# The opening of a convolution by Fourier tables: where k is turned, and on which engines the tables are made

## The chip, the cores and the metric

The kernel runs on one core of a Trainium2 chip. A core has five engines, each with a queue of its own: TensorE (PE, matrix products; PEld is its weight load), VectorE (DVE), ScalarE (ACT), GpSimd (POOL) and SyncE (SP, which here only issues transfers). They work on the on-chip memory SBUF (128 partitions) and on PSUM, where matrix products land. The metric is device time in microseconds for one execution, the median of several.

## The reference, cut to what matters

A forward pass of four layers and its gradients are computed, for 2048 positions and 512 channels. Two layers are a convolution A over the positions and two a dense layer B with GELU:

```python
def _A_ref(q, k, v, shift_k, ssm_k, ssm_D):
    k_pad = jnp.pad(k, ((0, 0), (ks - 1, 0), (0, 0)))
    k_shift = jnp.zeros_like(k)
    for t in range(ks):                       # ks = 4
        k_shift = k_shift + k_pad[:, t:t + S, :] * shift_k[:, ks - 1 - t][None, None, :]
    kv = k_shift * v
    # kv and ssm_k are padded to 4096, multiplied as spectra, and transformed back: y
    y = y + kv * ssm_D[None, None, :]
    return q * y

x = A_q
x = x + _A_ref(_layernorm(x), A_k, A_v, ...)
x = x + _B_ref(_layernorm(x), B_w1, ...)
x = x + _A_ref(_layernorm(x), A_k, A_v, ...)
x = x + _B_ref(_layernorm(x), B_w1, ...)
```

The gradients of all inputs but B_x are returned too. k, v and ssm_k are the same in both A layers, so y is computed once.

## The kernel before, in words

`phase_conv_forward` computes y, `phase_mlp` runs the layers forward and back, and `conv_backward` with `weight_grads` does the rest. The change lies in the first 85 us, in `phase_conv_forward`.

The Fourier transforms are products with tables of sines and cosines. The 2048 frequencies are split into five `GROUPS` by residue, and each group has its own folding of the input (`Fold.streams`), so that a group needs two or four streams of 512 columns times 128x128 pieces of table.

The opening has these steps, in the order of the code:

- **h chunks** (`h_chunk`, called from the loop at L518, four times). ssm_k, called h, is turned (transposed by a product with the identity) 128 channels at a time. One half goes to `ha_ps` in PSUM and is copied to `hA` by VectorE; the other to `hb_ps` and is copied to `hR` by ScalarE (L513). The four middle taps go through `hs_ps` to `hsp`. Ahead of each chunk `sin_of` (L175) makes one quarter of the table `tabN`. It works on 1024 columns at a time: a phase (frequency times position plus a shift, in integers), an AND with 8191, and a sine on ScalarE (L186). The phase of the first 1024 columns is made on GpSimd (L182) and that of the second on VectorE; both ANDs are on VectorE. The three buffers of `tab_u` hold the phases until their sine is done.
- **wdiag** (L526): sixteen diagonal matrices with the shift taps, on VectorE.
- **hB** (L531 to L533): `hR` is reversed by eight products with the anti-diagonal `anti` into `hr_ps`, and copied to `hB` by ScalarE.
- **tap rows** (L534 to L541): the table rows `sp5` for the middle taps and ssm_D, by ten calls of `sin_of` on 5 partitions and 128 columns each (five groups, cosine and sine).
- **fold of h** (L545 to L547): one row of `hB` is set to zero, then `Fold` and the streams of groups 0 and 1, `sth`, on VectorE.
- **k slices** (`k_slice`, L468, called four times at L583). 512 positions of k, loaded to `kns`, are turned by four sets of four products into `kt_ps` (two buffers of one PSUM bank, tag `kt`), each copied to `kT` by ScalarE (L475). Small copies on GpSimd (L477, L479) join the edges of neighbouring slices.
- **shift products** (`ks_slice`): k_shift by 64 products of `kT` with `wdiag` per slice, into `ks_ps`, copied by ScalarE to `ksb` (L492), stored, and multiplied by v on VectorE into `kv`, which is kept in `y_res`. Between them come `h_group`(0) and (1), the spectrum of h for the first two groups, the streams of the later groups, and `tabF_part`, which makes the table `tabF` for kv with the same `sin_of`. After them the other h groups run, with the turning of both tables in between (`table_turns`), and the spectrum of kv follows.

The h groups (`fwd_group`) use `sp_ps`, two buffers of two PSUM banks each (tag `sp`). Each of their results sums a real and an imaginary part; the first block of group 0 needs `sp5` and `altq` in its imaginary part (`extra`, L549). [...]

What sets the order: `nc = Ordered(...)` (L415) keeps the instructions of TensorE and VectorE in the order in which the code writes them, in this phase. L55 is the line of that wrapper, so all their rows have L55 in the profile and are told apart by their tiles. The order on ScalarE, GpSimd and SyncE, and of every engine in `phase_mlp`, is written by a planner, which takes the instruction that it reckons ready, the earlier one in the code first. Every engine then works its queue in that fixed order.

Of the kernel before, what the change touches and what calls it, by code (L numbers as in the profile page):

```python
# [11 lines left out]
ACT = mybir.ActivationFunctionType  # L12
ALU = mybir.AluOpType
BF16 = mybir.dt.bfloat16
F32 = mybir.dt.float32
I32 = mybir.dt.int32
P = 128
# [54 lines left out]
def ssm_kernel(ctx, tc: tile.TileContext, aps: dict):  # L72
# [28 lines left out]
    dram.gp = {li: drampool.tile([P, NFC, S], BF16, name=f"gp{li}_d") for li in (1, 3)}  # L101
    res.wstack = ExitStack()
    phase_conv_forward(nc, tc, dims, consts, dram, res, aps)
    flip_rows(nc, dram.goB, aps["grad_out"].flatten_outer_dims(), 511)
    with ExitStack() as res.gystack:
# [17 lines left out]
GROUPS = [(0, 0, 2), (4, 2, 2), (2, 4, 4), (1, 8, 4), (3, 12, 4)]  # L123


def iota_f32(nc, pool, shape, pattern, base, mult, name):
    ti = pool.tile(shape, I32, name=name + "_i")
    nc.gpsimd.iota(ti, pattern=pattern, base=base, channel_multiplier=mult)
    tf = pool.tile(shape, F32, name=name)
    nc.vector.tensor_copy(out=tf, in_=ti)  # L130
    return tf
# [40 lines left out]
SIN_SCALE = -(2.0 * math.pi / 8192.0) * (1.0 - SIN_EPS)  # L172


def sin_of(nc, consts, pool, out, krow, pv, shift, np_=P):  # L175
    n = krow.shape[-1]
    us = []
    for c0 in range(0, n, 1024):
        w = min(1024, n - c0)
        u = pool.tile([P, 1024], I32, name="tab_u", tag="tab_u", bufs=3)[0:np_, 0:w]  # L180
        eng = nc.gpsimd if c0 == 0 else nc.vector
        eng.tensor_scalar(out=u, in0=krow[:, c0:c0 + w], scalar1=pv, scalar2=float(shift), op0=ALU.mult, op1=ALU.add)  # L182
        us.append((c0, w, u))
    for c0, w, u in reversed(us):
        nc.vector.tensor_single_scalar(out=u, in_=u, scalar=8191, op=ALU.bitwise_and)
        nc.scalar.activation(out=out[:, c0:c0 + w], in_=u, func=ACT.Sin, scale=SIN_SCALE, bias=consts.pibias[0:np_, :])  # L186
# [105 lines left out]
def fwd_group(nc, psum, tab, st, g, out, extra=None, m0=0, m1=None, c0=0):  # L292
    k1, base, n = GROUPS[g]
    for mt in range(m0, n if m1 is None else m1):
        cols = slice((base + mt) * P - c0, (base + mt + 1) * P - c0)
        ps = psum.tile([P, 2, 512], F32, name="sp_ps", tag="sp", bufs=2)
        R, Z = [], []
        for qt in range(2):
            C, S = tab[:, 0, qt, cols], tab[:, 1, qt, cols]
            q = slice(qt * 512, (qt + 1) * 512)  # L300
            if k1 in (0, 4):
                R.append((C, st["e"][:, q]))
                Z.append((S, st["o"][:, q]))
            else:
                R += [(C, st["er"][:, q]), (S, st["oi"][:, q])]
                Z += [(C, st["nei"][:, q]), (S, st["orr"][:, q])]
        if extra is not None:
            er, ez = extra(g, mt, st)
            R += er
            Z += ez  # L310
        for b, lst in ((0, R), (1, Z)):
            for i, (a, r) in enumerate(lst):
# [97 lines left out]
def phase_conv_forward(ctx, nc, tc, dims, consts, dram, res, aps):  # L410
    S, D, NT, ND = dims.S, dims.D, dims.NT, dims.ND
# [3 lines left out]
    nc = Ordered(nc, tc, ("tensor", "vector"))  # L415
    tt = nc.vector.tensor_tensor
    psum = ctx.enter_context(tc.tile_pool(name="cf_ps", bufs=1, space=bass.MemoryType.PSUM))
# [8 lines left out]
    tabF = tabs.tile([P, 2, 2, 2048], BF16, name="tabF")  # L426
# [4 lines left out]
    gp = gen.enter_context(tc.tile_pool(name="cf_gen", bufs=1))  # L431

    KA, KB, KW = 16, 272, 544
    kns = []
# [9 lines left out]
    krow = gp.tile([P, 2048], F32, name="krow")  # L444
# [4 lines left out]
    kT = gp.tile([P, ND, 4, KW], BF16, name="kT")  # L449
# [8 lines left out]
    hsp = gp.tile([5, D], BF16, name="hsp")  # L458
# [4 lines left out]
    pvh = iota_f32(nc, gp, [P, 2], [[2 * P, 2]], -511, 2, "pvh")  # L463
    pvn = iota_f32(nc, gp, [P, 2], [[2 * P, 2]], 0, 2, "pvn")
    tabN = gp.tile([P, 2, 2, 2048], BF16, name="tabN")
    sp5 = gp.tile([5, 5, 2, P], BF16, name="sp5")
    altq = gp.tile([P, P], BF16, name="altq")
    def k_slice(i):  # L468
        for h in range(4):
            ps = psum.tile([P, ND, P], F32, name="kt_ps", tag="kt", bufs=2)  # L470
            for cc in range(ND):
                nc.tensor.matmul(ps[:, cc, :], lhsT=kns[i][:, h, cc * P:(cc + 1) * P],
                                 rhs=consts.ident if h < 2 else consts.anti, start=True, stop=True)
            c0 = KA + P * h if h < 2 else KB + P * (3 - h)
            nc.scalar.activation(out=kT[:, :, i, c0:c0 + P], in_=ps, func=ACT.Identity)  # L475
        for j in range(1, 4):
            nc.gpsimd.tensor_copy(out=kT[:, :, i, KB + 255 + j:KB + 256 + j], in_=kT[:, :, i, KA + 256 - j:KA + 257 - j])  # L477
            if i < 3:
                nc.gpsimd.tensor_copy(out=kT[:, :, i + 1, KA - j:KA + 1 - j], in_=kT[:, :, i, KB + j - 1:KB + j])  # L479
# [20 lines left out]
    def h_chunk(cc):  # L500
        b = cc * S
        for m in range(2):
            c = slice(m * 512 + cc * P, m * 512 + (cc + 1) * P)
            ps = psum.tile([P, 4, P], F32, name="ha_ps", tag="kt", bufs=2)
            for i in range(4):
                nc.tensor.matmul(ps[:, i, :], lhsT=hN[:, b + 512 * i + m * P:b + 512 * i + m * P + P], rhs=consts.ident,
                                 start=True, stop=True)
            nc.vector.tensor_copy(out=hA[:, :, c], in_=ps)
            ps = psum.tile([P, 4, P], F32, name="hb_ps", tag="ks", bufs=2)
            for i in range(4):  # L510
                t0 = b + 512 * (i or 4) - m * P - P + 1
                nc.tensor.matmul(ps[:, i, :], lhsT=hN[:, t0:t0 + P], rhs=consts.ident, start=True, stop=True)
            nc.scalar.activation(out=hR[:, :, c], in_=ps, func=ACT.Identity)  # L513
        ps = psum.tile([4, P], F32, name="hs_ps", tag="kt", bufs=2)
        nc.tensor.matmul(ps, lhsT=hN[:, b + 256:b + S:512], rhs=consts.ident, start=True, stop=True)
        nc.vector.tensor_copy(out=hsp[0:4, cc * P:(cc + 1) * P], in_=ps)

    for cc in range(ND):  # L518
        qt, f = cc // 2, cc % 2
        sin_of(nc, consts, gp, tabN[:, f, qt, :], krow, pvn[:, qt:qt + 1], 2048 * (1 - f))  # L520
        h_chunk(cc)
    wshf = gp.tile([P, ND, 4], F32, name="wshf")
    nc.vector.tensor_copy(out=wshf, in_=wsh)
    for cc in range(ND):
        for j in range(4):
            nc.vector.tensor_scalar(out=wdiag[:, cc, j, :], in0=consts.ident, scalar1=wshf[:, cc, j:j + 1],  # L526
                                    scalar2=None, op0=ALU.mult)

    for m in range(2):
        for i in range(4):  # L530
            ps = psum.tile([P, 512], F32, name="hr_ps", tag="ks", bufs=2)  # L531
            nc.tensor.matmul(ps, lhsT=consts.anti, rhs=hR[:, i, m * 512:(m + 1) * 512], start=True, stop=True)
            nc.scalar.activation(out=hB[:, i, m * 512:(m + 1) * 512], in_=ps, func=ACT.Identity)  # L533
    pi5 = gp.tile([5, 1], I32, name="pi5")  # L534
    nc.vector.memset(pi5, 0)
    nc.gpsimd.iota(pi5[0:4, :], pattern=[[0, 1]], base=512, channel_multiplier=1024)
    pv5 = gp.tile([5, 1], F32, name="pv5")
    nc.vector.tensor_copy(out=pv5, in_=pi5)
    for gi, (k1, base, n) in enumerate(GROUPS):
        for f in range(2):  # L540
            sin_of(nc, consts, gp, sp5[:, gi, f, :], krow[0:5, base * P:(base + 1) * P], pv5, 2048 * (1 - f), np_=5)  # L541
    nc.vector.memset(sp5[:, 0, 1, 0:1], 1.0)
    nc.vector.memset(altq, 0.0)
    nc.vector.tensor_copy(out=altq[:, 0:1], in_=consts.alt)
    nc.vector.memset(hB[0:1, :, 0:512], 0.0)  # L545
    fh = Fold(nc, foldp, hA, hB, True, xpool=res.xpool)
    sth = [fh.streams(GROUPS[0][0]), fh.streams(GROUPS[1][0])]  # L547

    def extra(g, mt, st):  # L549
        R = [(sp5[:, g, 0, :], hsp)]  # L550
        Z = [(sp5[:, g, 1, :], hsp)]
        if g == 0:
            Z = []
            if mt == 0:
                Z = [(sp5[:, g, 1, :], hsp), (altq, st["e"][:, 0:512]), (altq, st["e"][:, 512:1024])]
        return R, Z

    tabIt = {}
# [16 lines left out]

    def tabF_part(x):
        qt, f = x // 2, x % 2
        sin_of(nc, consts, gp, tabF[:, f, qt, :], krow, pvh[:, qt:qt + 1], 2048 * (1 - f))
        if f:
            nc.vector.tensor_copy(out=tabF[:, 1, qt, 0:1], in_=consts.alt)  # L580

    for i in range(4):
        k_slice(i)  # L583
    for i in range(4):
        ks_slice(i)
        if i < 2:
            h_group(i)
        if i in (1, 3):
            sth.append(fh.streams(GROUPS[(i + 3) // 2][0]))
        tabF_part(i)  # L590
# [881 lines left out]
```

## Time and profile before

| | |
|---|---|
| median of 10 runs | 927.1 us (924.51 to 935.75) |
| the profiled execution | 928.26 us |
| its span, first to last instruction | 926.5 us |
| mean granted TensorE clock | 0.94 |
| PE busy | 774.8 us (84%) |
| VectorE busy | 733.5 us (79%) |
| ScalarE busy | 568.3 us (61%) |
| GpSimd busy | 150.9 us (16%) |

How to read the lines shown: a timeline row has the start in us, the time from the first to the last instruction of the row, the engine, the line of the code, the operation, the tile written and the tiles read, shapes, and xN for N instructions merged. In brackets stands how long the engine had been idle and what released it. A row of the table by stretches has, for each engine, the busy time in that stretch and the number of instructions, then the granted TensorE clock, the share of the transfer engines and the transfer rate. The windows of such a table cut off at a time, so neighbouring rows add up.

### The profile page before, as it was taken

The page shows a single profiled execution, that of the slowest core. Times are in us where ns is not written, and L with a number is a line of the kernel's source. Part 1 is how long each engine was busy: PE and PEld are TensorE (multiplying, and loading weights), DVE is VectorE, ACT ScalarE, POOL GpSimd, SP SyncE. Part 2 cuts the span into 40 slices and gives each one's busy share as a digit, 9 for nine tenths or more (in the row PEclk, how much of TensorE's full clock was granted, in tenths as well). Part 3 has the DMA queues.
Part 4 walks back from the last instruction along what each step waited for, and adds up shares of the span by engine and source line. Part 5 has one row for each costly group of instructions (what it writes and reads, how often), then busy time and mean ns, then how long its engine had stood idle before and what let it go on. Part 6 is the DMA issues. An engine that isn't in the chain of part 4 may idle for free. (4 is left out here: it accounts for less than half of the span.)

```text
span 926.5 us, 12075 instructions
## 1 busy us (share of the span) xinstructions
PE 774.8 (84%) x4329; PEld 387.0 (42%) x4402; DVE 733.5 (79%) x1203; ACT 568.3 (61%) x742; POOL 150.9 (16%) x274
## 2 busy tenths in 40 slices
PE   3688878964788658657999999997999998898997
PEld 2463323431333223223444444442344445765664
DVE  7747589797899988965837877898569999899774
ACT  5867554645998898686973655632533316754664
POOL 6632210012001010100001122221010222310000
PEclk9998998987999788978999999997999999999999
DMA  6568868312435534646689786756979998884321
GB/s 218 184 236 307 303 241 284 105 46 62 140 116 160 162 118 135 192 126 191 215 290 291 194 233 197 232 167 156 272 214 261 220 360 299 270 288 107 100 76 39
DMA packets 200580, 180.82 MB, mean 195 GB/s; under 512 B 95749, under 2 KB 182984, under 8 KB 200136
## 3 DMA queue, kind: packets, MB, share of 16 engines
q1 hardware_dynamic: 185320, 133.60, 49.7%
q0 software_dynamic: 11968, 40.15, 12.6%
q10 hardware_dynamic: 3232, 6.29, 1.9%
q8 instruction: 34, 0.56, 0.2%
q14 instruction: 26, 0.21, 0.1%
HBM read 84.22 MB, written 82.13 MB: 180 GB/s over the span
## 5 line engine op out<-in xcount | busy, mean ns | idle before, releaser
L55 PE MATMUL dw_ps<-G,dw_tm 128*128 128x512 bf16 x679 | 164.7, 387 | 8.8 <-ACT dw_tm L1263 3.8
L1096 PE MATMUL z_ps<-nT_sl,w_sb 128*128 128x512 bf16 x345 | 93.8, 429 | 46.7 <-DMA nT_sl<-n_sl 32.2
L1107 PE MATMUL o_ps<-w_sb,h_sl 128*128 128x512 bf16 x344 | 89.5, 398 | 30.2 <-DVE h_sl L1078 27.3
L55 PEld LDWEIGHTS <-dw_tm 128*128 128x128 bf16 x704 | 67.5, 100 | 81.7 <-issue 6.3
L1126 ACT ACTIVATE gz_sl<-gh_ps 128x512 bf16<-128x512 f32 x88 | 50.4, 594 | 56.6 <-PE gh_ps L1124 56.6
L1143 PE MATMUL gn_ps<-w1T_sb,gz_sl 128*128 128x512 bf16 x348 | 80.8, 379 | 0.7 <-DVE gz_sl L1127 0.5
L1096 PEld LDWEIGHTS <-w_sb 128*128 128x128 bf16 x352 | 37.4, 108 | 101.0 <-issue 55.2
L1124 PE MATMUL gh_ps<-gT_sl,w2T_sb 128*128 128x512 bf16 x341 | 78.3, 379 | 0.5
L1098 ACT ACTIVATE g_z<-z_ps,b1col 128x512 bf16<-128x512 f32 x88 | 55.3, 712 | 27.7 <-PE z_ps L1096 27.7
L1107 PEld LDWEIGHTS <-h_sl 128*128 128x128 bf16 x352 | 34.8, 102 | 78.3 <-DVE h_sl L1078 35.1
L1263 ACT ACTIVATE dw_tm<-dw_tp 128x1024 bf16<-128x1024 bf16 x44 | 44.6, 1024 | 27.4 <-PE dw_tp L55 23.3
L1143 PEld LDWEIGHTS <-gz_sl 128*128 128x128 bf16 x352 | 34.4, 98 | 42.1 <-DVE gz_sl L1127 1.0
L1124 PEld LDWEIGHTS <-w2T_sb 128*128 128x128 bf16 x352 | 34.3, 98 | 41.2
L55 DVE TENSOR_REDUCE b1a<-dw_fm 128x1 f32<-128x2048 bf16 x22 | 49.6, 2277 | 0.0
L998 POOL TENSOR_SCALAR rstd<-ln_mv 128x4 f32<-128x4 f32 x16 | 7.5, 469 | 249.9 <-DVE ln_mv L996 161.9
L1155 POOL TENSOR_SCALAR bb_diag<-ident,bb_cols 128x128 bf16<-128x128 bf16 x32 | 20.9, 652 | 156.0 <-DVE bb_junk L1152 146.8
L1127 DVE TENSOR_TENSOR gz_sl<-gz_sl,gpb 128x2048 bf16<-128x2048 bf16 (+1 forms) x24 | 27.2, 1135 | 23.3 <-ACT gz_sl L1126 11.5
L1074 ACT ACTIVATE g_s<-g_t 128x2048 bf16<-128x2048 bf16 (+1 forms) x24 | 42.8, 1785 | 2.5 <-DVE g_t L1073 2.4
L1322 ACT ACTIVATE dw_o<-dw_ps 128x512 bf16<-128x512 f32 x22 | 13.1, 596 | 49.3 <-PE dw_ps L55 29.4
L1078 DVE TENSOR_TENSOR h_sl<-g_s,g_z 128x2048 bf16<-128x2048 bf16 (+1 forms) x24 | 27.2, 1131 | 20.4 <-ACT g_s L1074 20.4
L1071 ACT ACTIVATE g_q<-g_z 128x2048 bf16<-128x2048 bf16 (+1 forms) x24 | 43.2, 1800 | 0.1
L1075 ACT ACTIVATE g_o<-g_t 128x2048 bf16<-128x2048 bf16 (+1 forms) x24 | 42.7, 1780 | 0.0
(299 smaller groups left out, 1634.4 us busy)
## 6 DMA issues: line engine op xcount, KB each, us to landing
dw_fm<-gz_d SPq DMA_DIRECT2D x22, 512.0 KB, 6.2
h_d<-h_sl SPq DMA_DIRECT2D x16, 512.0 KB, 3.0
gp_d<-g_p SPq DMA_DIRECT2D x16, 512.0 KB, 3.3
nb_sl<-n_d SPq DMA_DIRECT2D x16, 512.0 KB, 4.4
gpb<-gp_d SPq DMA_DIRECT2D x16, 512.0 KB, 5.1
gz_d<-gz_sl SPq DMA_DIRECT2D x16, 512.0 KB, 4.3
n_d<-n_sl SPq DMA_DIRECT2D x12, 512.0 KB, 3.3
Hspec_d<-Hg ACTq DMA_DIRECT2D x8, 512.0 KB, 4.9
```

The source lines that it names most:

```text
L55: return self.tc.keep_in_program_order(f(*args, **kwargs))
L1071: nc.scalar.activation(out=q, in_=zb, func=ACT.Square)
L1074: nc.scalar.activation(out=sg, in_=t, func=ACT.Sigmoid)
L1075: nc.scalar.activation(out=o, in_=t, func=ACT.Sigmoid, scale=-1.0)
L1078: nc.vector.tensor_tensor(out=h, in0=sg, in1=zb, op=ALU.mult)
L1096: nc.tensor.matmul(ps, lhsT=w.w1[:, dc, c * P:(c + 1) * P], rhs=nT[:, dc, :], start=(dc == 0), stop=(dc == ND - 1))
L1098: nc.scalar.activation(out=zb[:, c - c0, :], in_=ps, func=ACT.Identity, bias=w.b1col[:, c:c + 1])
L1107: nc.tensor.matmul(ps, lhsT=h[:, c, t * P:(t + 1) * P], rhs=w.w2[:, c, :], start=(c == 0), stop=False)
L1124: nc.tensor.matmul(ps, lhsT=w.w2T[:, dc, c * P:(c + 1) * P], rhs=gT[:, dc, :], start=(dc == 0), stop=(dc == ND - 1))
L1126: nc.scalar.activation(out=gz[:, c, :], in_=ps, func=ACT.Identity)
L1143: nc.tensor.matmul(ps, lhsT=gz[:, c, t * P:(t + 1) * P], rhs=w.w1T[:, c, :], start=(c == 0), stop=(c == NFC - 1))
L1263: nc.scalar.activation(out=dst, in_=ps, func=ACT.Identity)
```

## The change

Four things are done.

1. `sin_of` takes an engine, and the phases of `tabN`, the tap rows and `tabF` are all made on VectorE.
2. `k_slice` turns two blocks of 128 positions into one buffer of the tag `sp`, 1024 columns, and copies them with one ScalarE instruction: two such halves for a slice. It no longer uses `kt`.
3. Slices 0 and 1 are turned after h chunks 2 and 3, and slices 2 and 3 after the products that reverse `hR`, ahead of the tap rows in the code.
4. The tap rows are made in two passes of 640 columns (one cosine, one sine for all five groups) from a copy `krow5` of the frequencies; `sp5` is laid out to match. The three small instructions that finish `sp5` and `altq` come after the two first folds.

```diff
-def sin_of(nc, consts, pool, out, krow, pv, shift, np_=P):
+def sin_of(nc, consts, pool, out, krow, pv, shift, np_=P, eng=None):
...
-        eng = nc.gpsimd if c0 == 0 else nc.vector
-        eng.tensor_scalar(out=u, in0=krow[:, c0:c0 + w], scalar1=pv, scalar2=float(shift), op0=ALU.mult, op1=ALU.add)
+        (eng or (nc.vector if c0 else nc.gpsimd)).tensor_scalar(out=u, in0=krow[:, c0:c0 + w], scalar1=pv, scalar2=float(shift), op0=ALU.mult, op1=ALU.add)
...
-    sp5 = gp.tile([5, 5, 2, P], BF16, name="sp5")
+    sp5 = gp.tile([5, 2, 5 * P], BF16, name="sp5")
...
     def k_slice(i):
-        for h in range(4):
-            ps = psum.tile([P, ND, P], F32, name="kt_ps", tag="kt", bufs=2)
-            for cc in range(ND):
-                nc.tensor.matmul(ps[:, cc, :], lhsT=kns[i][:, h, cc * P:(cc + 1) * P],
-                                 rhs=consts.ident if h < 2 else consts.anti, start=True, stop=True)
-            c0 = KA + P * h if h < 2 else KB + P * (3 - h)
-            nc.scalar.activation(out=kT[:, :, i, c0:c0 + P], in_=ps, func=ACT.Identity)
+        for flip in range(2):
+            ps = psum.tile([P, 2, 512], F32, name="kt_ps", tag="sp", bufs=2)
+            for x in range(2):
+                h = 3 - x if flip else x
+                for cc in range(ND):
+                    nc.tensor.matmul(ps[:, x, cc * P:(cc + 1) * P], lhsT=kns[i][:, h, cc * P:(cc + 1) * P],
+                                     rhs=consts.anti if flip else consts.ident, start=True, stop=True)
+            c0 = KB if flip else KA
+            nc.scalar.activation(out=kT[:, :, i, c0:c0 + 2 * P].rearrange("p c (h q) -> p c h q", h=2),
+                                 in_=ps[:, :, :].rearrange("p h (c q) -> p c h q", c=ND), func=ACT.Identity)
...
     for cc in range(ND):
         qt, f = cc // 2, cc % 2
-        sin_of(nc, consts, gp, tabN[:, f, qt, :], krow, pvn[:, qt:qt + 1], 2048 * (1 - f))
+        sin_of(nc, consts, gp, tabN[:, f, qt, :], krow, pvn[:, qt:qt + 1], 2048 * (1 - f), eng=nc.vector)
         h_chunk(cc)
+        if cc >= 2:
+            k_slice(cc - 2)
...
+    for i in range(2, 4):
+        k_slice(i)
+    krow5 = gp.tile([P, 1024], F32, name="krow5", tag="tab_u", bufs=3)[0:5, 0:5 * P]
+    for gi, (k1, base, n) in enumerate(GROUPS):
+        nc.vector.tensor_copy(out=krow5[:, gi * P:(gi + 1) * P], in_=krow[0:5, base * P:(base + 1) * P])
     pi5 = gp.tile([5, 1], I32, name="pi5")
...
-    for gi, (k1, base, n) in enumerate(GROUPS):
-        for f in range(2):
-            sin_of(nc, consts, gp, sp5[:, gi, f, :], krow[0:5, base * P:(base + 1) * P], pv5, 2048 * (1 - f), np_=5)
-    nc.vector.memset(sp5[:, 0, 1, 0:1], 1.0)
-    nc.vector.memset(altq, 0.0)
-    nc.vector.tensor_copy(out=altq[:, 0:1], in_=consts.alt)
+    for f in range(2):
+        sin_of(nc, consts, gp, sp5[:, f, :], krow5, pv5, 2048 * (1 - f), np_=5, eng=nc.vector)
     nc.vector.memset(hB[0:1, :, 0:512], 0.0)
     fh = Fold(nc, foldp, hA, hB, True, xpool=res.xpool)
     sth = [fh.streams(GROUPS[0][0]), fh.streams(GROUPS[1][0])]
+    nc.vector.memset(sp5[:, 1, 0:1], 1.0)
+    nc.vector.memset(altq, 0.0)
+    nc.vector.tensor_copy(out=altq[:, 0:1], in_=consts.alt)
...
     def tabF_part(x):
         qt, f = x // 2, x % 2
-        sin_of(nc, consts, gp, tabF[:, f, qt, :], krow, pvh[:, qt:qt + 1], 2048 * (1 - f))
+        sin_of(nc, consts, gp, tabF[:, f, qt, :], krow, pvh[:, qt:qt + 1], 2048 * (1 - f), eng=nc.vector)
...
-    for i in range(4):
-        k_slice(i)
     for i in range(4):
         ks_slice(i)
```

`extra` takes its rows from the new layout of `sp5`; nothing else changes.

More of the change, by code (lines that the diff above doesn't have):

```diff
@@ L547, in phase_conv_forward @@
     sth = [fh.streams(GROUPS[0][0]), fh.streams(GROUPS[1][0])]
+    nc.vector.memset(sp5[:, 1, 0:1], 1.0)
+    nc.vector.memset(altq, 0.0)
+    nc.vector.tensor_copy(out=altq[:, 0:1], in_=consts.alt)
     def extra(g, mt, st):
-        R = [(sp5[:, g, 0, :], hsp)]
-        Z = [(sp5[:, g, 1, :], hsp)]
+        R = [(sp5[:, 0, g * P:(g + 1) * P], hsp)]
+        Z = [(sp5[:, 1, g * P:(g + 1) * P], hsp)]
         if g == 0:
@@ L554, in extra @@
             if mt == 0:
-                Z = [(sp5[:, g, 1, :], hsp), (altq, st["e"][:, 0:512]), (altq, st["e"][:, 512:1024])]
+                Z = [(sp5[:, 1, g * P:(g + 1) * P], hsp), (altq, st["e"][:, 0:512]), (altq, st["e"][:, 512:1024])]
         return R, Z
```

## The prediction

> **What bounds the kernel now.** The page's chain that ended last covers only the final 77 us (dw, gh), so it says nothing of the opening. I read next the busy time by stretch, to see which engine is full where the change acts:
>
> ```profile
> core 0: us, PE busy (x) PEld busy (x) DVE busy (x) ACT busy (x) POOL busy (x), PEclk, DMA share, GB/s
> 6.60:25.00 18.40, 7.55 (x59) 5.86 (x58) 15.07 (x24) 13.13 (x17) 9.17 (x14) 1.00 0.60 201
> 25.00:37.95 12.95, 6.72 (x32) 3.29 (x31) 6.29 (x35) 11.55 (x25) 6.67 (x19) 1.00 0.59 194
> 37.95:49.90 11.95, 10.80 (x108) 9.16 (x107) 9.15 (x6) 8.43 (x16) 10.12 (x18) 1.00 0.41 155
> 49.90:69.30 19.40, 17.02 (x214) 12.43 (x215) 9.73 (x10) 12.66 (x18) 6.26 (x5) 1.00 0.73 267
> ```
>
> Until 25 us VectorE leads (15.07 of 18.40) and PE is mostly idle; then ScalarE (11.55 of 12.95); from 37.95 PE. So PE has room early for work that it does late. The timeline of VectorE shows why the fold starts only at 37.95:
>
> ```profile
> 11.26 0.69 DVE L55 TENSOR_SCALAR tab_u<-tab_u 128x1024 int32<-128x1024 int32 x1 [3.19 <-POOL tab_u L182]
> 14.03 2.10 DVE L55 TENSOR_SCALAR tab_u<-tab_u 128x1024 int32<-128x1024 int32 x2
> 22.40 1.29 DVE L55 TENSOR_SCALAR tab_u<-tab_u 128x1024 int32<-128x1024 int32 x2
> 25.00 0.15 DVE L55 CAST wshf<-wsh 128x16 f32<-128x16 bf16 x1
> 29.10 0.14 DVE L55 CAST pv<-pi 5x1 f32<-5x1 int32 x1 [1.22 <-POOL pi L536]
> 33.45 0.21 DVE L55 TENSOR_SCALAR tab_u<-tab_u 5x128 int32<-5x128 int32 x1 [2.44 <-POOL tab_u L182]
> 37.00 0.91 DVE L55 MEMSET hB<- 1x1024 uint32 x1
> 37.95 4.49 DVE L55 TENSOR_TENSOR fold_x<-hA,hB 128x4096 bf16<-128x4096 bf16 x2
> 44.80 2.36 DVE L55 TENSOR_TENSOR fold_t<-fold_s 128x2048 bf16<-128x2048 bf16 x2
> ```
>
> A wait of 3.19 for POOL in the first chunk; then from 29 to 36.6 ten tap-row steps of 0.21 each, waiting 5.2 us in all for POOL. ScalarE and PE over the same time:
>
> ```profile
> 29.83 1.09 ACT L533 ACTIVATE hB<-hr_ps 128x512 bf16<-128x512 f32 x2 [0.18 <-PE hr_ps L55]
> 32.58 0.97 ACT L186 ACTIVATE sp<-tab_u,pibias 5x128 bf16<-5x128 int32 x3
> 33.70 3.32 ACT L186 ACTIVATE sp<-tab_u,pibias 5x128 bf16<-5x128 int32 x7 [0.15 <-DVE tab_u L55]
> 36.92 1.05 ACT L475 ACTIVATE kT<-kt_ps 128x512 bf16<-128x512 f32 x2
> 37.54 0.59 PE L55 MATMUL kt_ps<-ident,kn 128*128 128x128 bf16 x4 [4.23 <-ACT kT L475]
> 44.27 4.95 PE L55 MATMUL ks_ps<-wdiag,kT 128*128 128x128 bf16 x64
> 49.91 0.60 PE L55 MATMUL sp_ps<-fold_t,tabN 128*128 128x512 bf16 x2
> ```
>
> hB is complete at 30.92; it is VectorE that comes 6 us later. The tap-row sines sit between kT evictions and hold PE for 4.23. PE starts the shift products at 44.27 and the imaginary part of the first h group at 49.91, my marker: from there nothing is edited but the tabF phases.
>
> **What the Trainium skill says.** "SBUF — State Buffer", Who interferes with whom: VectorE in a two-port mode and GpSimd exclude each other. The trace agrees: the pair of AND steps takes 2.10 with POOL busy, 1.29 without. "TensorE: Matmul & The Clock Gate", Engine queue depths: ScalarE and VectorE queues are strict FIFO; the hB memset at 37.00 agrees, late behind the tap rows. "ScalarE: Activation LUTs", What ACT_TABLE_LOAD costs: with a pointer bias 280 + 0.833 N ns, with immediates 186 + 0.833 N. The trace has 1142 ns for the sine of 1024 (page: 1133), 1020 for a 128x1024 eviction (1039). For 5x640, which no row shows, the page gives 813 ns.
>
> **The change, part by part.** Times are on the profiled execution's span of 926.5.
>
> *Table phases on VectorE.* One more 128x1024 phase per chunk, 0.73 (start to start about 0.7). The last chunk, with POOL idle, runs 21.63 to 25.00 = 3.37; so 4.1 per chunk, against 6.68, 4.18, 4.18, 3.37 before. The first starts at 6.59, so wshf comes at 6.59 + 4 x 4.1 = 23.0: 2.0 earlier. The three buffers of tab_u suffice while sines keep up, and ScalarE has 3.4 us of sines and hR per chunk. Four tabF phases add 0.75 each after 49.91; before, the next VectorE work was a kv product waiting 4.56 for ScalarE, later 4.14 for a tabF sine, so they are covered; uncovered they cost 3.0. POOL loses all of it, its 3.51 us step at 58.50 too.
>
> *Tap rows in two passes.* After 23.0: wshf and wdiag 2.9, five copies of 5x128 about 0.7, the pi5/POOL/pv5 step 1.0 (1.4 before), then two passes of phase (between 0.21 at 128 and 0.73 at 1024: 0.51) and AND (0.49): 2.0. VectorE is free for hB's memset at 29.6, 7.4 earlier. Moving the sp5 and altq fixes behind the streams puts 0.4 after them.
>
> *k between the chunks.* Per slice sixteen matmuls at 0.48 per four (38.81 to 39.30) = 1.95 of PE, and two evictions of 128x1024 at 1.02 (start to start 0.95) for four at 0.54: nearly equal. The sp buffers are unused before 49, so the first slice waits for nothing but kn, issued by 7.1 and 9.9 to landing, so there by 17. Chunk 2's hs lies 0.73 behind its first hA copy, which starts 2.75 into the chunk at 14.8: 18.3. PE turns slice 0 from 18.5 to 20.5, chunk 3 then still has its ha at 21.0, before VectorE wants it (21.6). Slice 1 goes to PE behind chunk 3's hs (22.4) and needs the sp buffers that ScalarE frees at 20.7 and 21.6: no wait; were there one, hr stands behind it in PE's queue, and hB and the fold wait for hr. POOL's queue takes the 21 small kT copies (0.15 each alone, up to 1.27 beside the fold) earlier; only ks and pi5's iota wait for POOL, the iota perhaps behind the wdiag store's 0.73 as now, which the 1.0 above covers. kT's store (2176 KB, behind the copies on POOL) moves from 48.5 into the stretch 44.3 to 49 in which DMA moved nothing, or ahead of it; SP's loads of v for products 0 and 1 are issued by 35 as before and landed when that stretch began.
>
> *ScalarE then decides.* Free of chunk 2's sines at 19.1, it has kT of slice 0 (19.7 to 21.6), two sines (to 23.8), two hR (24.9), kT of slice 1 (26.7), then eight hB at their old pace, 26.03 to 30.92 = 4.9: 31.6. The two tap-row sines are ready by 29.6 and I take them into hB's run as before into kT's: 2 x 0.72 less two gaps of 0.18 = 1.1. hB complete at 32.7, behind VectorE's 29.6; latency 0.1, memset 0.95: fold at 33.75 for 37.95. The streams end 9.2 later, the fixes at 43.4, PE's marker at 43.5 for 49.91: **6.4 us earlier**.
>
> *PE's other input.* Slices 2 and 3 follow hr (before, 0.84 ahead of hB's end): about 31.9, two slices 3.9 and 0.4 of waits: ks at 36.2 for 44.27, 8.1 earlier. It is not the later one.
>
> *Bounds.* ScalarE's last possible order before hB (all sines whole) ends hB at 33.1, the earliest (kT of slice 1 behind hB) at 30.3: gain 6.0 to 8.8, the upper end close to what ks allows. A loss of more than 0.4 in the opening is excluded, kn being there: from 19.7 all of ScalarE's work (kT 7.8, sines 3.6, hR 1.2, hB 4.9) is 17.5, ending at 37.2, so even with hB last of all the fold would start at 38.3.
>
> From the marker PE is 88% busy to 69.3 and VectorE then ScalarE and PE alternate to 214; loads there follow releases in the chain, so the shift is carried. Span 920.1. The profiled execution took 928.26, 1.76 more than its span and 1.16 above the median; the shift is taken off the median: 927.1 - 6.4 = **920.7 us**.
>
> **Rivals.** *Larger*: ScalarE's and PE's waits after the marker (0.6, 0.5, 1.1 for ks, 2.8 for the turns) come from where the planner puts tabF's sines; with POOL's late half gone they can fall too: 6.4 + 3 = 9.4, 917.7. Against: those waits name ScalarE's total load, which stays. *Given back*: ScalarE's order is planned anew and the sines land ahead of evictions PE waits for; one more wait each like the 2.8 and the 0.6 leaves 3.0: 924.1. For it: exactly this happened at 32.58. Against: ScalarE is 12.66 of 19.40 busy, with gaps. *Slower*: in the MLP the engines have only a planned order, and PE already waits 11.83 us at 224.5 for g_z and 8.29 at 310.6 for a transposed load. One more wait of the first kind: 927.1 - 6.4 + 11.8 = 932.5; it is slower by 0.5% from a wait of 11.1. Against: its inputs all shift together. *Doesn't do what it says*: kn lands after 18.5 and PE holds chunk 3; each us late is a us less; at 6.4 no gain, 927.
>
> **How the numbers follow.** A measurement tells about 0.5%, 4.6 us, from no change. Forecast (gain 4.6 to 8.8) 0.50; larger 0.10; given back, or kn late, 0.28; slower 0.12. Faster than 922.5 is the first two, 0.60; within, given back and a little of the slower case, 0.29; slower 0.11. The likeliest's own range is 918 to 922.5. Range 915 to 928: it takes in the larger gain and the given back and leaves out about 0.12 above and 0.05 below.
>
> **What would show it.** Right: VectorE's wshf near 23 with no wait on POOL in the chunks; k's matmuls between 18.5 and 25 without waits; two sp5 sines of about 0.8; fold_x near 33.8 with hB's memset waiting for ScalarE; ks near 36; the altq matmuls near 44. Wrong: hB later than 34, fold waiting on VectorE's own queue, new PE waits on ScalarE from 45 to 100, or a first z_ps (207.6 before) not some 6 us earlier; that row parts an opening gain lost in the conv from one lost in the MLP.

## The result and the profile after

The changed kernel took 917.11 us (median of 15 runs, 912.85 to 927.66), the kernel before on the same chip 926.63 (median of 52 runs). The ratio is 0.9891, with a 95% interval of 0.9871 to 0.9912: faster by 10.1 us of 926.63 (8.2 to 12.0). The forecast was 6.4. Executions of one and the same kernel are told apart into faster and slower ones (medians of 928.73 and 940.75 for the kernel before on one chip); the ratios compare the faster ones alone, and two of the profiles below (the changed kernel again, the ten tap rows without waits for buffers) are of slower ones.

The marker, PE's imaginary part of the first h group, moved from 49.91 to 39.91: 10.0 us, as much as the whole gain.

```profile
39.91 0.60 PE L55 MATMUL sp_ps<-fold_t,tabN 128*128 128x512 bf16 x2
```

The profiled execution of the changed kernel took 922.07 us, span 920.3, clock 0.94. Its busy time by stretch, cut at its own events (end of the chunks, start of the fold, marker, and 20 us more):

```profile
core 0: us, PE busy (x) PEld busy (x) DVE busy (x) ACT busy (x) POOL busy (x), PEclk, DMA share, GB/s
6.60:22.75 16.15, 9.08 (x86) 7.78 (x84) 16.01 (x29) 14.57 (x18) 7.64 (x16) 1.00 0.65 217
22.75:30.93 8.18, 4.90 (x28) 2.25 (x26) 6.54 (x30) 7.59 (x13) 1.79 (x8) 0.80 0.40 147
30.93:39.90 8.97, 6.24 (x90) 5.25 (x89) 8.90 (x5) 7.31 (x10) 7.85 (x7) 0.99 0.72 231
39.90:59.90 20.00, 17.09 (x213) 12.40 (x214) 10.94 (x16) 12.33 (x18) 2.71 (x7) 1.00 0.88 328
```

Three stretches got shorter: 18.40 became 16.15, 12.95 became 8.18, 11.95 became 8.97; 2.25 + 4.77 + 2.98 = 10.0. In the first, VectorE now works without a gap (16.01 of 16.15) and ScalarE nearly so (14.57). In the third, VectorE is full instead of PE: PE did part of its work on k before. The stretch behind the marker is loaded as before.

The 2.25 of the first stretch can be told apart by chunk: 6.68, 4.18, 4.18 and 3.37 became 4.05, 4.04, 4.04 and 4.04. The first chunk gained 2.63, the next two 0.14 each, and the last lost 0.67. In the first chunk of the kernel before, VectorE's wait of 3.19 was for a phase that GpSimd began only at 10.11, because ten small steps for another table (`col256`, 6.06 to 9.85) stood ahead of it in its queue. In the next two chunks the extra phase on VectorE cost nearly what the AND steps gained. Whether moving those ten steps, with the phases left on GpSimd, would have done as much was not tried.

VectorE's timeline, with the start, the time and the waits:

```profile
22.75 0.15 DVE L55 CAST wshf<-wsh 128x16 f32<-128x16 bf16 x1
27.48 0.14 DVE L55 CAST pv<-pi 5x1 f32<-5x1 int32 x1 [1.18 <-POOL pi L545]
27.73 0.54 DVE L55 TENSOR_SCALAR tab_u<-krow,pv 5x640 int32<-5x640 f32 x1
29.29 0.48 DVE L55 TENSOR_SCALAR tab_u<-tab_u 5x640 int32<-5x640 int32 x1
29.93 0.91 DVE L55 MEMSET hB<- 1x1024 uint32 x1 [0.16 <-DVE tab_u L55]
30.93 4.49 DVE L55 TENSOR_TENSOR fold_x<-hA,hB 128x4096 bf16<-128x4096 bf16 x2
37.79 2.36 DVE L55 TENSOR_TENSOR fold_t<-fold_s 128x2048 bf16<-128x2048 bf16 x2
```

The 3.19 wait for POOL in the chunks is gone; the tap rows take 2.0 instead of 7.5. The memset's 0.16 is VectorE's own queue, not ScalarE. The prediction had expected ScalarE there, and had named a fold that waits on VectorE's own queue among its signs of being wrong: this sign came.

ScalarE's timeline (its copies out of PSUM are called evictions from here on):

```profile
24.17 1.96 ACT L476 ACTIVATE kT<-kt_ps 128x1024 bf16<-128x1024 f32 x2
29.62 1.09 ACT L537 ACTIVATE hB<-hr_ps 128x512 bf16<-128x512 f32 x2 [0.18 <-PE hr_ps L55]
30.96 3.77 ACT L476 ACTIVATE kT<-kt_ps 128x1024 bf16<-128x1024 f32 x4 [0.26 <-PE kt_ps L55]
34.60 1.53 ACT L185 ACTIVATE sp<-tab_u,pibias 5x640 bf16<-5x640 int32 x2
```

hB is complete at 30.71. The two tap-row sines come four evictions later, at 34.60, although their input was ready at 29.8. And PE's:

```profile
18.25 1.03 PE L55 MATMUL kt_ps<-ident,kn 128*128 128x128 bf16 x8
33.40 1.95 PE L55 MATMUL ks_ps<-wdiag,kT 128*128 128x128 bf16 x32
36.66 1.95 PE L55 MATMUL ks_ps<-wdiag,kT 128*128 128x128 bf16 x32 [1.31 <-ACT ksb L494]
39.07 0.38 PE L55 MATMUL sp_ps<-fold_t,tabN 128*128 128x512 bf16 x1 [0.46 <-DVE fold_t L55]
```

Slice 0 of k is turned at 18.25 without a wait. The shift products start 10.9 us earlier, and PE then waits 0.46 for the first fold_t: the fold and the shift products arrive almost together.

**Behind the marker.** The single profiled executions differ more than the medians: the first z_ps product came at 195.1 for 207.6 (12.5 earlier), the end only 6.2 earlier. Most of the difference lies in the backward convolution. There VectorE waited 11.1 us, in two waits, for loads of Hb. Of two further executions of the changed kernel, below, one has this again and one has not.

### The profile page after: what moved, and what is told of

It reads as the page before. It is cut to its first block, busy times and chain, and to the rows that moved or that the text cites. A ratio compares the mean times of both kernels' runs of the same rounds, so it can differ in the third digit from the quotient of the medians.

```text
span 920.3 us, 12048 instructions
## 1 busy us (share of the span) xinstructions
PE 768.3 (83%) x4329; PEld 382.9 (42%) x4402; DVE 735.7 (80%) x1210; ACT 564.2 (61%) x726; POOL 137.4 (15%) x256
## 5 line engine op out<-in xcount | busy, mean ns | idle before, releaser
L1269 ACT ACTIVATE dw_tm<-dw_tp 128x1024 bf16<-128x1024 bf16 x44 | 44.6, 1024 | 27.3 <-PE dw_tp L55 24.6
```

The costliest lines, as they stand in the source:

```text
L1269: nc.scalar.activation(out=dst, in_=ps, func=ACT.Identity)
```

## The experiments

The parts are not independent, so each was undone alone in the changed kernel, and each was made alone in the kernel before. Starts are from the profiled executions, in us: of the fold of h (fold_x), of the shift products (ks) and of the marker. The last column is the time against the kernel before on the same chip, with its interval. The intervals of the changed kernel, of k late, of the table phases half on GpSimd and of the run without waits for buffers overlap, so what sets these four apart is read at the marker.

| kernel | fold_x | ks | marker | to before | ratio |
|---|---|---|---|---|---|
| before | 37.95 | 44.27 | 49.91 | | 1 |
| changed | 30.93 | 33.40 | 39.91 | -10.0 | 0.9891 [0.9871, 0.9912] |
| changed, k late | 30.35 | 35.91 | 41.31 | -8.6 | 0.9916 [0.9883, 0.9949] |
| changed, table phases half on GpSimd | 33.45 | 36.11 | 42.42 | -7.5 | 0.9924 [0.9889, 0.9959] |
| changed, ten tap rows | 42.61 | 33.20 | 52.22 | +2.3 | 1.0102 [1.0070, 1.0134] |
| the same, without waits for buffers | 33.89 | 33.40 | 42.90 | -7.0 | 0.9918 [0.9886, 0.9949] |
| before, table phases alone | 35.04 | 41.36 | 46.28 | -3.6 | 0.9976 [0.9939, 1.0012] |
| before, two-pass tap rows alone | 32.59 | 41.09 | 46.80 | -3.1 | 0.9957 [0.9919, 0.9994] |
| before, k alone | 46.00 | 36.33 | 55.61 | +5.7 | 1.0076 [1.0049, 1.0103] |

**The changed kernel again**, unedited.

> The changed kernel once more, as the control for the three beside it. Both theories: the marker (PE's imaginary part of the first h group) at 39.9 and the first z_ps of the MLP near 195, as in its first profile, so 10 to 12.5 us ahead of the kernel before. Where the profiled execution gave about 7 us back between 686 and 707 us (VectorE waiting 11.1 us for Hb, PE's clock at 0.66) I expect this not to recur: then the span is 913 to 915. If it belongs to the change, it recurs and the span is near 920.

Ratio 0.9900 [0.9829, 0.9970]; fold 30.94, ks 33.19, marker 39.91. The opening repeats to 0.01 us at the fold and the marker. The long stretch of the backward inverse transform came again (679.6 to 739.2, 59.6 us for 52.0 before), against the expectation, and the span was 927.9, above both cases. That left open whether the stretch belongs to the change; the last run of this section bears on it.

**k late**: all four slices behind the tap rows, with the new wide evictions kept.

```diff
-        if cc >= 2:
-            k_slice(cc - 2)
...
-    for i in range(2, 4):
-        k_slice(i)
...
+    for i in range(4):
+        k_slice(i)
     for i in range(4):
         ks_slice(i)
```

> The changed kernel with all four k slices back ahead of the shift products; taps, phases and the sp buffers as changed. Theory A (what sets the gain is when VectorE starts the fold, k need only be out of the way): hB's run loses the four kT evictions ahead of it, but the fold stays at 30.9, set by VectorE's own queue; eight kT evictions of 0.93 and the two tap-row sines follow hB, ks starts near 36 for 33.4, the marker falls from 39.9 to 41.8 and the time is 1.9 us above the changed kernel's. Theory B (k's place between the chunks is the gain): ks returns to 41 or later, the marker to 46 to 48, the time 6 to 8 us above.

```profile
26.90 0.14 DVE L55 CAST pv<-pi 5x1 f32<-5x1 int32 x1 [0.60 <-POOL pi L541]
35.91 4.72 PE L55 MATMUL ks_ps<-wdiag,kT 128*128 128x128 bf16 x64
```

The marker came 1.4 later than in the changed kernel, at 41.31: near theory A. hB was done earlier, at 28.0, having no k eviction ahead of it. The fold started 0.6 earlier, not because of hB but because VectorE waited 0.60 instead of 1.18 for GpSimd's iota, ahead of which no kT copies stood here. ks started 2.5 later and set the marker. So with the two other parts in place, k's place between the chunks is worth only 1.4. The tap rows' sines lay in this kernel between k's evictions, at 29.9 and 31.5; two of 0.81 hurt little.

**Ten tap rows**: the two passes undone, with the phases of the ten on GpSimd as before.

```diff
-    krow5 = gp.tile([P, 1024], F32, name="krow5", tag="tab_u", bufs=3)[0:5, 0:5 * P]
...
-    for f in range(2):
-        sin_of(nc, consts, gp, sp5[:, f, :], krow5, pv5, 2048 * (1 - f), np_=5, eng=nc.vector)
+    for gi, (k1, base, n) in enumerate(GROUPS):
+        for f in range(2):
+            sin_of(nc, consts, gp, sp5[:, f, gi * P:(gi + 1) * P], krow[0:5, base * P:(base + 1) * P], pv5, 2048 * (1 - f), np_=5)
```

> The changed kernel with the tap rows made by ten calls on 128 columns again, their phases on GpSimd; the rest as changed. Theory A: VectorE enters the tap rows at 25.5 and takes the 9.2 us that it took before (27.83 to 37.00): fold at 35.7 for 30.9, marker at 44.7, time 4.8 us above the changed kernel's. Theory B: with k already turned the sines no longer hold PE, and the cost is 1 us or less.

This expectation fell by 7.5 us: the fold started at 42.61, later than in the kernel before, and the marker came at 52.22. VectorE's timeline has two long waits among the ten steps:

```profile
29.10 0.21 DVE L55 TENSOR_SCALAR tab_u<-tab_u 5x128 int32<-5x128 int32 x1 [0.27 <-POOL tab_u L181]
36.13 0.21 DVE L55 TENSOR_SCALAR tab_u<-tab_u 5x128 int32<-5x128 int32 x1 [6.81 <-POOL tab_u L181]
39.83 0.21 DVE L55 TENSOR_SCALAR tab_u<-tab_u 5x128 int32<-5x128 int32 x1 [2.51 <-POOL tab_u L181]
42.61 4.49 DVE L55 TENSOR_TENSOR fold_x<-hA,hB 128x4096 bf16<-128x4096 bf16 x2
```

The timelines of ScalarE and GpSimd in the same kernel have what the fourth row waited for:

```profile
30.77 3.77 ACT L476 ACTIVATE kT<-kt_ps 128x1024 bf16<-128x1024 f32 x4 [0.26 <-PE kt_ps L55]
34.40 0.97 ACT L185 ACTIVATE sp<-tab_u,pibias 5x128 bf16<-5x128 int32 x3
35.10 0.59 POOL L597 DMA_DIRECT2D kT_d<-kT  x1 [0.97 <-ACT sp L185]
35.73 1.33 POOL L181 TENSOR_SCALAR tab_u<-krow,pv 5x128 int32<-5x128 f32 x3
```

The waits come after three steps and after six, and `tab_u` is a ring of three buffers, used in turn. A fourth tap row can only be written once a sine has read the first. In this code k's slices 2 and 3 stand ahead of the tap rows, the planner puts their four evictions ahead of the sines, and so the sines start at 34.40. The chain is: eviction, sine, buffer, GpSimd's phase, VectorE's AND, memset, fold. So far that is a reading of the trace; the next run tests it.

**The same ten tap rows without the waits for buffers.** The steps write slices of two buffers that all hold at once.

```diff
+    tu = [gp.tile([P, 1024], I32, name="tab_u", tag="tab_u", bufs=3) for f in range(2)]
     for gi, (k1, base, n) in enumerate(GROUPS):
         for f in range(2):
-            sin_of(..., np_=5)
+            sin_of(..., np_=5, own=tu[f][0:5, gi * P:(gi + 1) * P])
```

> The run with ten tap rows (phases on GpSimd), whose steps here write slices of two tab_u buffers, so that no tap row waits for another's sine to give a buffer back; all else as there. If the loss of that run (fold_x 42.61, marker 52.22) is the wait for buffers behind sines that stand after k's evictions, VectorE now runs the ten steps at 0.49 each from 28.1: memset at 32.9, fold_x at 33.8 to 34.0, marker at 42.8 to 43.0, some 7 us below the kernel before as with phases on GpSimd. If ten small steps handed over from GpSimd are themselves what is slow, fold_x stays above 40 and the marker above 49.

```profile
32.51 0.21 DVE L55 TENSOR_SCALAR tab_u<-tab_u 5x128 int32<-5x128 int32 x1 [0.27 <-POOL tab_u L181]
33.89 4.53 DVE L55 TENSOR_TENSOR fold_x<-hA,hB 128x4096 bf16<-128x4096 bf16 x2
34.60 3.01 ACT L185 ACTIVATE sp<-tab_u,pibias 5x128 bf16<-5x128 int32 x10
42.90 0.61 PE L55 MATMUL sp_ps<-fold_t,tabN 128*128 128x512 bf16 x2
```

The fold started at 33.89 and the marker came at 42.90, both inside what was written. Same engines, same ten steps, same ten sines, which the planner still put behind k's evictions (at 34.60, all ten together): 9.3 us less at the marker, 8.7 of them at the fold. So it was the waits for buffers; that GpSimd's ten phases now ran ahead of kT's copies follows from it. Of the two passes, then, 3.0 us (42.90 against 39.91) are due to fewer, larger steps on one engine, and the other 9.3 to needing no buffer back: ten rows turn over a ring of three, while the two passes take just three buffers (`krow5` is one). The prediction named only the first kind.

The times agree in sign (1.0102 and 0.9918) but not in size: 18.4 thousandths are 17 us, at the marker they are 9.3. Part of what is lost with ten rows is PE's pace after the long wait. PE had stood idle for 12.90, and the first products came slowly:

```profile
50.74 0.59 PE L55 MATMUL sp_ps<-fold_t,tabN 128*128 128x512 bf16 x1 [12.90 <-DVE fold_t L55]
52.22 1.03 PE L55 MATMUL sp_ps<-fold_t,tabN 128*128 128x512 bf16 x2
```

A pair took 1.03 instead of 0.60, and the granted clock was 0.50 from 51 to 56 us. This is 0.6 of the 9.3 at the marker, and by the third h group's first product the two kernels are 11.8 apart (74.45 and 62.65). By the first z_ps it is 10.6 again (209.6 and 199.0). What the rest of the loss is stays open. Its profile has 12.3 us of waits for loads of Hb and KVb in the backward convolution, but the changed kernel's has 11.1 for Hb as well, with a time of 0.9891.

**Table phases half on GpSimd**, as before, in the changed kernel.

```diff
-        sin_of(nc, consts, gp, tabN[:, f, qt, :], krow, pvn[:, qt:qt + 1], 2048 * (1 - f), eng=nc.vector)
+        sin_of(nc, consts, gp, tabN[:, f, qt, :], krow, pvn[:, qt:qt + 1], 2048 * (1 - f))
...
-        sin_of(nc, consts, gp, tabF[:, f, qt, :], krow, pvh[:, qt:qt + 1], 2048 * (1 - f), eng=nc.vector)
+        sin_of(nc, consts, gp, tabF[:, f, qt, :], krow, pvh[:, qt:qt + 1], 2048 * (1 - f))
```

> The changed kernel with the first phase of every table quarter, tabN and tabF, on GpSimd again; the tap rows stay on VectorE. Theory A: VectorE waits 3.2 us in the first chunk and runs its AND steps beside GpSimd at 2.10 for 1.29; wshf at 25.0 for 22.75, the fold and the marker 2.2 us later, time 2.2 us above the changed kernel's, all of it from tabN. Theory B: PE and ScalarE are held by hR and kT either way, marker within 0.5 us, and what GpSimd takes from VectorE in the four tabF parts shows later or not at all.

wshf came at 25.18, 2.43 later than in the changed kernel, and the marker 2.5 later. What the chunks lose reaches the marker whole. The wait in the first chunk was there again, 3.20 long.

**k alone** in the kernel before.

```diff
     def k_slice(i):
-        for h in range(4):
-            ps = psum.tile([P, ND, P], F32, name="kt_ps", tag="kt", bufs=2)
+        for flip in range(2):
+            ps = psum.tile([P, 2, 512], F32, name="kt_ps", tag="sp", bufs=2)
...
         h_chunk(cc)
+        if cc >= 2:
+            k_slice(cc - 2)
...
+    for i in range(2, 4):
+        k_slice(i)
     pi5 = gp.tile([5, 1], I32, name="pi5")
...
-    for i in range(4):
-        k_slice(i)
     for i in range(4):
         ks_slice(i)
```

> The kernel before with k's part alone: two blocks to a buffer, slices 0 and 1 between the h chunks, 2 and 3 behind hr; the tables' phases stay half on GpSimd and the tap rows ten. From the run with ten tap rows (fold_x at 42.61, marker 52.22) I expect that the tap rows' sines fall behind k's evictions in ScalarE's planned order here too, so that VectorE waits some 7 us for tab_u buffers: wshf at 25, fold_x at 44 to 45, ks early (36), the marker at 53 to 55 for 49.91 before, time 3 to 5 us above the kernel before. Rival: the parts add, and k alone is worth the time ks comes earlier: the marker at 46 to 48, 2 to 4 us below the kernel before.

```profile
39.26 0.21 DVE L55 TENSOR_SCALAR tab_u<-tab_u 5x128 int32<-5x128 int32 x1 [7.55 <-POOL tab_u L182]
46.00 4.50 DVE L55 TENSOR_TENSOR fold_x<-hA,hB 128x4096 bf16<-128x4096 bf16 x2
```

The wait after three tap rows is there again, 7.55 long. ks started 7.9 us earlier than before and PE then stood idle for 13.16 until the fold's first result. The marker came 5.7 later than before, 0.6 beyond what was expected, and the time was 7.1 us longer (0.76%). The part that gives PE its early work is, alone, a loss: as in the run with ten tap rows, it puts k's evictions ahead of the sines on which the fold depends through the buffers.

**Two-pass tap rows alone.**

```diff
+    krow5 = gp.tile([P, 1024], F32, name="krow5", tag="tab_u", bufs=3)[0:5, 0:5 * P]
...
-    for gi, (k1, base, n) in enumerate(GROUPS):
-        for f in range(2):
-            sin_of(nc, consts, gp, sp5[:, gi, f, :], krow[0:5, base * P:(base + 1) * P], pv5, 2048 * (1 - f), np_=5)
+    for f in range(2):
+        sin_of(nc, consts, gp, sp5[:, f, :], krow5, pv5, 2048 * (1 - f), np_=5, eng=nc.vector)
```

> The kernel before with the tap rows in two passes alone (their phases on VectorE, as the change has them), tables half on GpSimd, k behind all. VectorE is then done early: fold_x at 33 to 34 for 37.95. But k's evictions follow the tap rows, so ks comes at 40.8 to 42 for 44.27 and PE, no longer the fold, sets the marker: 46.5 to 47.6 for 49.91, time 2.3 to 3.4 us below the kernel before. If the fold alone set the marker it would be at 42 to 43, 7 to 8 us below.

The fold started at 32.59, 5.4 earlier; ks at 41.09, 3.2 earlier, after a row of k evictions with gaps of at most 0.20. The marker, at 46.80, followed ks. With the fold alone it would by estimate have been at 41.6 (32.59 + 8.98, as in the changed kernel): without k's new place 5.2 of 8.3 us are given away again.

**Table phases alone.**

> The kernel before with all table phases on VectorE alone; the tap rows (ten, phases on GpSimd) and k stay. wshf at 22.8 to 23.0 for 25.00, hB, tap rows and fold all about 2.2 earlier: fold_x near 35.8, marker near 47.7, time about 2.2 us below the kernel before. Rival: ten tap rows wait for sines that the planner puts elsewhere, and nothing of the 2.2 is left at the marker (49.5 to 50).

```profile
30.54 0.21 DVE L55 TENSOR_SCALAR tab_u<-tab_u 5x128 int32<-5x128 int32 x1 [1.73 <-POOL tab_u L181]
```

wshf came at 22.76, the fold 2.9 earlier at 35.04, ks 2.9 earlier, the marker 3.6 earlier at 46.28: more than forecast. Beyond the 2.2 of wshf the fold gained 0.7 at the fourth tap row, whose wait fell from 2.44 to 1.73. ks itself also took 4.24 instead of 4.95 from start to end. The time's interval (0.9939 to 1.0012) takes in both the 3.6 and nothing.

**Is the memset behind hB's last eviction?** The halves of hr in the other order, so that the half that the memset clears is written last.

```diff
-    for m in range(2):
+    for m in (1, 0):
```

> The changed kernel with the halves of hr in the other order, so that the half of hB that the memset clears is written last. The prediction had taken the memset of 0.95 as serial behind hB's last eviction, while in the changed kernel's trace it starts at 29.93, before hB's last eviction ends at 30.71. If that is why the fold came at 30.93 and not 31.8, the memset here waits for ScalarE to 30.7 to 30.8 and fold_x starts at 31.7 to 31.8, 0.8 later; the marker follows by 0.4 to 0.8 (PE's own work holds it to 39.45 at the earliest). If not, fold_x stays at 30.9 to 31.0.

```profile
30.77 0.91 DVE L55 MEMSET hB<- 1x1024 uint32 x1 [0.99 <-ACT hB L537]
31.71 4.49 DVE L55 TENSOR_TENSOR fold_x<-hA,hB 128x4096 bf16<-128x4096 bf16 x2
```

Now the memset waits for ScalarE and the fold starts 0.78 later; the marker came at 40.69, also 0.78 later. So in the changed kernel the memset runs beside hB's second half because it touches only the first half, which is written first.

**Which of hB and VectorE holds the fold?** The tap rows' column of frequencies moved up to the other columns, to take the 1.18 wait for GpSimd off VectorE's way.

```diff
     pvn = iota_f32(nc, gp, [P, 2], [[2 * P, 2]], 0, 2, "pvn")
+    pi5 = gp.tile([5, 1], I32, name="pi5")
+    nc.vector.memset(pi5, 0)
+    nc.gpsimd.iota(pi5[0:4, :], pattern=[[0, 1]], base=512, channel_multiplier=1024)
+    pv5 = gp.tile([5, 1], F32, name="pv5")
+    nc.vector.tensor_copy(out=pv5, in_=pi5)
```

> The changed kernel with the column of frequencies of the tap rows (memset, GpSimd's iota, copy) moved up to the other columns, so that VectorE has no wait of 1.18 for GpSimd at 27.5. VectorE comes to the memset at about 28.8; the fold then waits for hB's last eviction at 30.71, so fold_x starts at 30.75 to 30.85 for 30.93 and the marker at 39.7 to 39.9: nearly nothing, because hB and VectorE arrive together. If VectorE alone set the fold, it would start at 29.8 and the marker at 39.4, where PE's own work holds it.

```profile
9.17 0.14 DVE L55 CAST pv<-pi 5x1 f32<-5x1 int32 x1 [2.73 <-POOL pi L465]
33.36 4.49 DVE L55 TENSOR_TENSOR fold_x<-hA,hB 128x4096 bf16<-128x4096 bf16 x2 [0.90 <-ACT hB L542]
```

As a step forward it failed: GpSimd put the new iota behind ten small steps of its own (6.06 to 8.8), VectorE waited 2.73 at the front, and all behind it came 2.84 later (wshf 25.59 for 22.75). As an answer it serves: relative to that, the fold came 0.4 earlier, and its last wait was 0.90 for hB. With the GpSimd wait out of the way hB is the last input, with it VectorE's queue is. The two are within half a microsecond of each other.

**The changed kernel a third time.**

> The changed kernel again. In two of its profiled executions the stretch of the backward inverse transform took 59 us for 52, with VectorE waiting 11.1 and 15.6 us for the loads of Hb. If that belongs to the change it comes again (last inverse product some 6 us earlier than before although the first is 13 earlier); if it varies with the execution, this profile can show 52 us. The opening as before: fold_x 30.9, marker 39.9, time 8 to 11 us below the kernel before.

Ratio 0.9886 [0.9807, 0.9964], fold 30.94, marker 39.91. The rows of the backward inverse transform, with its first and last start, first in the first profile of the changed kernel:

```profile
L55 PE MATMUL iv_ps<-Yb,tabIb x110: 379/379/634, 675.2 to 734.6; 128*128 128x512 bf16 x110
```

and in this one:

```profile
L55 PE MATMUL iv_ps<-Yb,tabIb x110: 379/379/379, 678.4 to 730.4; 128*128 128x512 bf16 x110
```

59.4 against 52.0, the latter just as before, and here VectorE waits for no load of Hb. The loads took 6.6 us to land in the median here, 8.6 in the first profile. So the loss varies from execution to execution of one and the same kernel. Nor does it need the whole change: the kernel before with the table phases alone has a stretch of 54.9, with 8.5 of waits for Hb. Whether it is commoner in the changed kernel than before three profiles can't tell; the medians leave little room for a lasting one: 10.0 at the marker, 10.1 at the end (8.2 to 12.0).

## Why the prediction was right, and where its sizes were off

The direction was right, the mechanism was right in the main, and the time fell into the range of 915 to 928. It did not fall into the range of the likeliest case (918 to 922.5, a gain of 4.6 to 8.8): the opening gained 3.6 us more than forecast, through terms of the sum that were too large. Term by term:

| term of the sum | predicted | measured | differs by |
|---|---|---|---|
| hB's run ends, without sines in it | 31.6 | 30.71 | 0.9 |
| tap-row sines inside hB's run | +1.1 | 0 (at 34.60) | 1.1 |
| memset and latency behind hB | +1.05 | +0.22 | 0.8 |
| fold_x starts | 33.75 | 30.93 | 2.8 |
| from fold_x to the marker | 9.75 | 8.98 | 0.8 |
| marker | 43.5 | 39.91 | 3.6 |

*Table phases on VectorE*: right. 4.04 per chunk for 4.1; wshf at 22.75 for 23.0. Undone alone it costs 2.5 at the marker, against the 2.0 of the sum. The Trainium skill's "SBUF — State Buffer", Who interferes with whom, was used rightly: the AND pair takes 1.29 to 1.30 in all four chunks, for 2.10 beside POOL. But this is not where the gain comes from: the 0.8 that each pair saves pays for the extra phase (0.7), and what is left is the first chunk's wait behind GpSimd's ten small steps.

*Tap rows in two passes*: the durations were right. Two passes took 2.04 (forecast 2.0), the copies 0.75 (0.7), the memset started at 29.93 (VectorE free at 29.6). The two sines, put at 813 ns by an estimate, took 0.81 each where they ran singly (k late). What was missing is the buffers. The prediction saw that before, ten steps waited for POOL and sines sat among k's evictions, and put the whole wait down to POOL. Of that wait 2.44 stood at the fourth row alone: GpSimd made its phase at 33.05, after the first sine at 32.58 had given a buffer back. The prediction did not ask what would become of ten rows in a ring of three once k's evictions stood ahead of the sines; with ten rows the whole change would have been a loss. That the two passes need no buffer back was luck as far as the prediction goes.

*k between the chunks*: right. Slice 0 was on PE at 18.25 and slice 1 at 22.23, without waits (forecast 18.5 and 22.4); the wide evictions started about 0.92 apart (0.95).

*ScalarE then decides*: half right. hB's end and VectorE's queue arrive together, and so ScalarE alone does not decide. Of the 2.8 that the fold came earlier than forecast, 0.9 is pace: the chunks were 0.25 earlier, one hR eviction came ahead of the two last sines, and hB's run took 4.73. The 1.1 was a wrong guess of the planner's order: the prediction carried over "as before into kT's" to hB's run, but the sines were put behind kT. The 0.8 was a wrong dependence: "latency 0.1, memset 0.95" was added behind hB's end. The memset writes hB's columns 0 to 511, which ScalarE finishes four evictions before the end. The code shows it (`hB[0:1, :, 0:512]` and the loop of halves outside the loop of slices); the swapped halves confirmed it, with 0.78.

*The fixes and the marker*: "The streams end 9.2 later, the fixes at 43.4, PE's marker at 43.5" put the marker behind both streams and the three fixes. The streams did end 9.2 after the fold's start, but PE's first group product needs only the first of the two fold_t steps, so it started 8.14 after it and the marker 0.84 later. The fixes, from 40.09 on, were needed only behind the marker, by the product with sp5 at 40.45 and the altq products at 40.76.

*PE's other input*: ks was forecast at 36.2, came at 33.40, and was "not the later one" by only 0.46 (0.67 in the second execution, no wait shown in the third). The runs with k late or k unchanged show that it becomes the later one at once.

*Bounds and the path behind*: the upper bound of 8.8 was too low, since it kept the serial memset and the late marker; these two alone add 1.6. The bound on a loss counted ScalarE's work and no wait for a buffer; the ten rows, with the fold at 42.61, show that such a wait can break it. That the shift is carried to the end was right in the medians.

*The rivals*: the larger gain, 917.7, has nearly the measured time, but not by its mechanism. PE's waits for ksb behind the marker did not fall (2.9 in all for 2.2), nor did the turns' wait (3.1 for 2.8). Its time was met because the forecast's own terms were too large. The sines did land elsewhere, as "given back" has it, but to PE's advantage. The slower rival did not occur: PE's waits for g_z were 14.3 in all for 14.1, and those for the transposed loads 32.0 for 32.2. kn was there in time.

## What to carry to other kernels

Where a chain runs through a ring of few buffers, ask which instruction gives the buffer back and what the planner will put ahead of that one; moving other work earlier in the code can delay it, here by 9.3 us. Follow a wait to the columns that an instruction really touches, and to the first of several merged steps that its reader needs, before calling it serial. The worth of parts that feed two inputs of one join does not add up: alone -3.6, -3.1 and +5.7 us at the marker here, together -10.0. Not tried here: a ring of more buffers, or the ten rows ahead of k in the code, which could have removed the same waits.

## What the runs show of the hardware

An AND on 5 partitions and 640 columns takes 0.48 us, on 5 by 128 it takes 0.21 and on 128 by 1024 it takes 0.69: the time follows the columns (0.53 ns for each further column from 128 to 640), not the partitions, so that five narrow steps cost more than one wide. The prediction had reckoned with this (0.49). GpSimd's copies of 128x4, 0.15 us each by themselves, took 4.60 for three beside VectorE's fold in the run without buffer waits, more than the 1.27 each that the prediction had seen; kT's store stood behind them there. Not expected was PE's pace after a long wait: idle for 12.90 with ten tap rows, it then had a granted clock of 0.50 from 51 to 56 us and of 1.00 from 60 to 64.
